# Sliding-window attention beside an MLP: fewer transfers for rows of maxima and outputs, and the last stage normalised a unit ahead

## The chip, the cores and the metric

The kernel runs on one core of a Trainium2 chip. Its metric is the device time of one execution in microseconds (us), the median of three runs. Five engines work side by side, each through its own queue in program order: PE (TensorE, matrix products; a matmul and the load of its weights are listed apart, as PE and PEld), DVE (VectorE), ACT (ScalarE), POOL (GpSimd) and SP (SyncE), which in this kernel only issues DMA transfers, all of them. An engine waits for another one by a semaphore; what stands behind a waiting instruction on the same engine waits with it.

## The reference

For x of shape [2048, 640], the layer norm `xn` of x goes two ways, and the result is `x + s * g`:

```python
qkv = (xn @ wqkv).reshape(B, S, 3, H, Dh)            # H = 32 heads of Dh = 20
scores = einsum("bhqd,bhkd->bhqk", q, k) * Dh ** -0.5
mask = (i - j >= 0) & (i - j < 256)                  # sliding window, causal
o = einsum("bhqk,bhkd->bhqd", softmax(where(mask, scores, -1e9)), v)
s = o.transpose(...).reshape(B, S, D) @ wo
h = relu(xn @ w1 + b1) ** 2                          # F = 1536
g = silu(h @ w2 + b2)
out = x + s * g
```

All inputs are float32. The kernel splits the operands of the large products into a rounded part (`fp32r`) and a remainder and sums three products of these, so that most products come in threes.

## The kernel before, in words

**Phase 1** normalises x in four blocks of 512 rows, transposes it, and makes v for all heads and q, k for the first head group. Results go to DRAM: q and k to `q_d`, `k_d`, v to `v_d`, the transposed x to `xs`.

**The attention** runs over 16 pairs of heads and, in each pair, 16 tiles of 128 query rows: 256 steps, and 11 more to drain. A step multiplies q with up to three tiles of keys (`sps`, L478), and DVE finds the maximum of each query (L486). Every fourth step (`max_rows`, L488) PE turns the maxima of four tiles into rows, ACT and POOL make a rounded row and a remainder of them (`mrow`, L500 and L501), and DMA writes these as two more rows under q for each head of the pair, in the tile `qs`. Nine steps later the scores are computed again with keys and queries exchanged (`stps`, L520); the two extra rows of q and rows of ones under k subtract the maximum in the product itself. ACT takes the exponential, POOL masks, and every fourth step `values` (L534) multiplies by v, with a column of ones that gives the sum of each softmax. For each of the two heads and for even and odd tiles the result `ot` lies in a group of 32 partitions, 21 of them used; ACT copies it to `osb`, and DMA takes it to `o_d`, one tensor for each block of 512 rows.

**The filler** puts everything else into the gaps of these steps: q and k of the other four head groups, then the MLP. The MLP has two halves of F and four blocks each; a block makes the hidden layer (`hps`) and then, for each of four tiles of rows and two halves of columns, a product `yps`, which DVE evicts with a sum (`ysb`, L953) to `y_d`. In the second half the first half's result comes back as `yin` (L877). A model clock orders the work: each product has a cost in `COST`, each group of value products `PV`, and `fill` issues filler products until the step's share of the model time is used up. The products are cut in two halves of 64 rows that run side by side on PE. A product needs one of three banks of PSUM, and the bank comes free by the eviction of the product that had it.

**The last stage** (`out_filler`, L1028) begins when the filler and all steps are through. It has eight units of 256 rows. `load` (L1000) brings a unit's attention output (`ob`), its softmax sums (`sums`, each row four times, since 128 partitions hold 32 heads four times over) and its MLP result (`yb`). `normalized` (L1034) takes the reciprocal, multiplies and splits in two pieces (DVE and ACT). Then for two tiles of 128 rows and two halves of columns 15 matmuls with `wo` fill a bank (`wops`, L602); DVE multiplies with the silu of `yb` (L1078), POOL adds x (L1079), and the row block goes out. `load` is called for units 0 and 1 in the last MLP block, after the second and the fourth of its tiles (L982). In the out stage, a unit is normalised ahead of the third of the four products of the unit before it; unit 0 is normalised at the start of the stage.

**Transfers on SP** stand in program order. `post` puts a transfer on a list and `post_all` (L567) issues the list: at the start of a step, after its filler work, and ahead of an eviction. Tiles have a fixed number of buffers; a transfer into one waits until its last reader is through.

## Time and profile before

| | |
|---|---|
| time, median of 3 runs | 927.04 us (922.24 to 929.7) |
| the profiled execution | 926.19 us, span 924.4 us |
| mean granted clock of PE | 0.983 |
| PE busy | 880.1 us (95%) |
| DVE, ACT, POOL busy | 498.9, 415.7, 327.1 us |
| moved by DMA | 165.76 MB, 179 GB/s over the span |
| transfers `qs<-mrow` | 256, 2 KB each |
| transfers `o<-osb` | 256, 21 KB each |
| transfers `sums<-o`, `ob<-o`, `yb<-y` | 32, 32 and 8 |

A row of the profile has the line, the engine, the operation, and the tiles as out<-in, with partitions x elements. The brackets at the end of a row in order of time give the idle time of the engine ahead of it and what ended it. A "granted clock" of 1.00 is the full clock of PE. Phase 1 takes about the first 115 us, the steps reach to about 800, and the last stage begins with the first `wops` at 831.9.

### The profile page before, as it was taken

How to read it: one execution, taken by the hardware profiler on the slowest of the kernel's cores; microseconds unless marked ns; L12 is line 12 of the kernel's file. 1: busy time of each engine (PE TensorE's matmuls, PEld its weight loads, DVE VectorE, ACT ScalarE, POOL GpSimd, SP SyncE). 2: the span in 40 equal slices, each digit the busy share in tenths (PEclk: the TensorE clock that was granted, in tenths of full speed). 3: DMA queues.
4: the chain of work that ended last, by engine and by line, in shares of the span. 5: the costliest groups of instructions: out<-in, count | busy, mean ns of one | idle time of the engine just before them, and what ended most of it. 6: DMA issues, size and time to landing. Idle time of an engine off the chain costs nothing. (4 is left out here: it accounts for less than half of the span.)

```text
span 924.4 us, 27328 instructions
## 1 busy us (share of the span) xinstructions
PE 880.1 (95%) x10640; PEld 815.5 (88%) x10640; DVE 498.9 (54%) x1446; ACT 415.7 (45%) x800; POOL 327.1 (35%) x702
## 2 busy tenths in 40 slices
PE   8999999999999999999999999999999999969887
PEld 8999999877878999989989899989899998958877
DVE  7652155655564655555555676745555653225664
ACT  4222125444454654644635656635635635502221
POOL 5010003232323543533534534534634534302223
PEclk9999999999998999999999999999999999988999
DMA  7996777677777453262365255465274532274984
GB/s 252 323 378 228 213 221 232 219 232 226 219 238 237 122 195 110 67 211 84 85 195 164 75 164 143 124 195 152 62 235 124 166 116 81 67 214 139 258 246 160
DMA packets 90825, 165.76 MB, mean 179 GB/s; under 512 B 11976, under 2 KB 46408, under 8 KB 88136
## 3 DMA queue, kind: packets, MB, share of 16 engines
q1 hardware_dynamic: 90696, 164.02, 57.2%
q8 instruction: 84, 1.38, 0.6%
q14 instruction: 45, 0.37, 0.1%
HBM read 94.71 MB, written 68.68 MB: 177 GB/s over the span
## 5 line engine op out<-in xcount | busy, mean ns | idle before, releaser
L486 DVE CUSTOM_DVE_ANT_0 junk<-sps,mask 128x384 bf16<-128x384 f32 (+2 forms) x512 | 271.8, 531 | 216.3 <-PE sps L478 82.9
L526 ACT ACTIVATE p<-stps 128x768 f32<-128x768 f32 (+2 forms) x256 | 197.1, 770 | 279.7 <-PE stps L520 234.3
L468 PE MATMUL yps<-w,hh 64*128 64x320 f32 x1536 | 231.4, 312 | 2.9 <-DVE sq L920 2.7
L527 POOL TENSOR_SCALAR_AFFINE_SELECT p<-p 128x256 f32<-128x256 f32 x256 | 104.6, 409 | 357.4 <-ACT p L526 354.2
L468 PE MATMUL hps<-xb,w 64*128 64x256 f32 x2520 | 220.7, 284 | 0.0
L468 PEld LDWEIGHTS hps<-xb,w 64*128 64x128 f32 x2520 | 207.9, 188 | 5.4 <-issue 5.1
L468 PEld LDWEIGHTS yps<-w,hh 64*128 64x128 f32 x1536 | 184.4, 186 | 8.2 <-DVE sq L920 4.6
L468 PE MATMUL yps<-w,hl 64*128 64x320 f32 x768 | 178.0, 311 | 0.0
L520 PE MATMUL stps<-qs,ks 62*128 62x384 f32 (+2 forms) x512 | 135.7, 339 | 15.5 <-DMA qs<-mrow 15.1
L478 PE MATMUL sps<-ks,qs 60*128 60x384 f32 (+2 forms) x512 | 139.1, 344 | 0.2
L468 PEld LDWEIGHTS yps<-w,hl 64*128 64x128 f32 x768 | 115.7, 186 | 2.5 <-issue 2.4
L520 PEld LDWEIGHTS stps<-qs,ks 62*128 62x128 f32 x512 | 86.6, 189 | 23.1 <-issue 16.1
L468 PE MATMUL qkps<-xT,wgkh 64*128 64x512 f32 x320 | 102.8, 406 | 0.0
L468 PE MATMUL qkps<-xT,wgqh 64*128 64x512 f32 x320 | 101.3, 398 | 0.0
L548 PE MATMUL ops<-p,vp 128*21 128x128 f32 (+1 forms) x2112 | 92.8, 313 | 0.0
L529 POOL TENSOR_SCALAR_AFFINE_SELECT p<-p 128x256 f32<-128x256 f32 x224 | 91.6, 409 | 0.0
L478 PEld LDWEIGHTS sps<-ks,qs 60*128 60x128 f32 x512 | 84.9, 187 | 2.9 <-DVE mt L486 1.7
L602 PE MATMUL wops<-wo,oT 128*128 128x320 f32 x384 | 69.4, 324 | 18.6 <-ACT oT L108 15.4
L548 PEld LDWEIGHTS ops<-p,vp 128*21 128x21 f32 x2112 | 65.2, 100 | 22.4 <-issue 9.5
L602 PEld LDWEIGHTS wops<-wo,oT 128*128 128x128 f32 x384 | 60.3, 196 | 23.9 <-ACT oT L108 17.9
L921 POOL TENSOR_TENSOR hl<-sq,hh 128x256 fp32r<-128x256 f32 x96 | 71.2, 744 | 23.1 <-DVE sq L920 20.5
L228 PE MATMUL vps<-wv,xT 128*128 128x320 f32 x480 | 71.5, 308 | 0.0
(99 smaller groups left out, 1221.1 us busy)
## 6 DMA issues: line engine op xcount, KB each, us to landing
ks<-k_d SPq DMA_DIRECT2D x64, 240.0 KB
qs<-q_d SPq DMA_DIRECT2D x64, 240.0 KB
xb<-xs SPq DMA_DIRECT2D x12, 1280.0 KB
xs<-xT SPq DMA_DIRECT2D x8, 1280.0 KB
y<-ysb SPq DMA_DIRECT2D x32, 320.0 KB
k_d<-shm SPq DMA_DIRECT2D x19, 512.0 KB
q_d<-shm SPq DMA_DIRECT2D x19, 512.0 KB
v_d<-vt SPq DMA_DIRECT2D x8, 672.0 KB
```

Source lines behind the costliest of these rows:

```text
L228: nc.tensor.matmul(ps, xT[xp][b][:, c * BT + t * P: c * BT + (t + 1) * P], wv[wp][:, c, nh * HALF:(nh + 1) * HALF], start=first and m == 0 ...
L468: return nc.tensor.matmul(out, a[r], b_[r], skip_group_check=True, **kw)
L478: nc.tensor.matmul(ss[hh][:, :nk], qs[i][o, q * P:(q + 1) * P], ks[i][o, k0 * P:k0 * P + nk], start=True, stop=True)
L486: nc.vector.tensor_tensor_reduce(out=junk[:, :nk], in0=ss[hh][:, :nk], in1=mask[:, 3 * P - nk:], scale=1.0, scalar=-3.0e38, op0=ALU.add, o ...
L520: nc.tensor.matmul(tps[:, hh, :n], ks[i][o, kb * P:(kb + 1) * P], qs[i][o, kb * P:kb * P + n], start=True, stop=True)
L526: nc.scalar.activation(p32[:, :, :n], tps[:, :, :n], AF.Exp, scale=SCALE)
L527: nc.gpsimd.affine_select(p32[:, :, 0:P], p32[:, :, 0:P], pattern=[[0, 2], [1, P]], compare_op=ALU.is_ge, fill=0.0, base=0, channel_multip ...
L529: nc.gpsimd.affine_select(p32[:, :, 2 * P:], p32[:, :, 2 * P:], pattern=[[0, 2], [-1, P]], compare_op=ALU.is_gt, fill=0.0, base=0, channel ...
L548: nc.tensor.matmul(ot[r0:r0 + VW, c0:c0 + len(part), :], vps[p][:, kb // 4, kb % 4, hh, :], pt[:, hh, :].rearrange("p (t n) -> p t n", n=P ...
L602: nc.tensor.matmul(ps, a, b_, start=j == 0, stop=j == n - 1)
L921: nc.gpsimd.tensor_sub(hh[1][:, sl], sq, f32(hh[0][:, sl]))
```

## The change

It has four parts.

1. The rows of maxima are written by two transfers for a group of four tiles, one for each of the two parts of `mrow`, each for both heads, and are issued at once instead of being posted.
2. The output of a block is written by one transfer of all 128 partitions, with the unused rows, into `o_d` of a new layout (row in the group, head, column). For that the groups of partitions in `ot` are exchanged: even and odd tiles of one head lie next to each other. So a unit is now two tiles of the same parity (`tile_of`), and its loads are three transfers instead of nine.
3. In the last MLP block `late` loads unit 0 at the start, and from the sixth of the eight products on issues the two pieces of unit 0's normalisation (`turn_out`) and the load of unit 1; it also takes up pieces of `wo`. In the last stage the two pieces of unit u+1 stand ahead of the first and the second product of unit u. The last tile's addition of x is on DVE.
4. `PV` is 1.57 instead of 1.65.

```diff
-PV = 1.65
+PV = 1.57
...
-    o_d = [dram.tile([H, VW, BT], F32, name=f"o_{g}") for g in range(NB)]
+    o_d = [dram.tile([2 * 32, H, MT], F32, name=f"o_{g}") for g in range(NB)]
...
-            for hh in range(2):
-                for a in range(2):
-                    o = hh * HP + KR + a
-                    post(f32(qs[i])[o:o + 1, g * 512:(g + 1) * 512].rearrange("r (q n) -> r q n", q=4), f32(mrow)[4 * hh:4 * hh + 4, a, :])
+            for a in range(2):
+                nc.sync.dma_start(f32(qs[i])[KR + a:KR + a + HP + 1:HP, g * BT:(g + 1) * BT].rearrange("h (q n) -> h q n", q=4), f32(mrow)[:, a, :])
...
-                    r0 = 32 * (hh + 2 * (t % 2))
+                    r0 = 32 * (2 * hh + t % 2)
...
-            for k in range(4):
-                post(o_d[g][2 * p + k % 2].rearrange("w (j e n) -> w j e n", j=2, e=2)[:, :, k // 2, :], osb[32 * k:32 * k + VW])
+            post(o_d[g][:, 2 * p:2 * p + 2, :].rearrange("r h n -> h r n"), osb.rearrange("p e n -> p (e n)"))
...
+        def late(j):
+            load(0)
+            if state[2] < 10 ** 6:
+                return
+            start_pieces()
+            for f in release(1, True):
+                f()
+                held[0] -= 1
+            if j >= 5:
+                turn_out(0, 0)
+            if j >= 6:
+                turn_out(0, 1)
+                load(1)
...
                 for nh in range(2):
                     yield from room()
+                    if n == last:
+                        late(2 * tt + nh)
                     job = start(nh)
...
-                if n == last and tt % 2:
-                    load(0)
-                    load(1)
...
+    def tile_of(u, t2):
+        return 4 * (u // 2) + u % 2 + 2 * t2
...
-        for k in range(4):
-            nc.sync.dma_start(sums[32 * k:32 * k + H], o_d[u // 2][:, DH, cols])
-            nc.sync.dma_start(ob[32 * k:32 * k + H], o_d[u // 2][:, k:DH:4, cols])
-        nc.sync.dma_start(yb, y_d[1][:, 2 * u:2 * u + 2, :])
+        rows = o_d[u // 2][32 * (u % 2):32 * (u % 2 + 1)]
+        nc.sync.dma_start(sums, rows[DH].unsqueeze(0).to_broadcast([4, H, MT]))
+        nc.sync.dma_start(ob, rows[:DH].rearrange("(c k) h n -> (k h) c n", k=4))
+        t = tile_of(u, 0)
+        nc.sync.dma_start(yb, y_d[1][:, t:t + 3:2, :])
...
+    def turn_out(u, part):
+        if (u, part) in turned_out or u not in ld:
+            return
+        turned_out.add((u, part))
+        ob, _, sums = ld[u]
+        if not part:
+            nc.vector.reciprocal(sums, sums)
+            big = bigp.tile([P, KC * BT], F32R, tag="big", name=f"oT_{u}")
+            oT[u] = big.rearrange("p (s c n) -> p s c n", s=2, c=KC)
+        cs = slice(2, KC) if part else slice(0, 2)
+        nc.vector.tensor_mul(ob[:, cs], ob[:, cs], sums.unsqueeze(1).to_broadcast([P, cs.stop - cs.start, MT]))
+        split(oT[u][:, 0, cs], oT[u][:, 1, cs], ob[:, cs])
...
-            if u not in oT:
-                flush()
-                normalized(u)
             flush()
+            turn_out(u, 0)
+            turn_out(u, 1)
...
-                    if t2 and not nh and u + 1 in ld:
+                    if not t2 and u + 1 in ld:
                         flush()
-                        normalized(u + 1)
+                        turn_out(u + 1, nh)
...
                         nc.vector.tensor_mul(res[:, sl], ps, yb[:, t2, sl])
+                        if t == NT - 1:
+                            nc.vector.tensor_add(res[:, sl], res[:, sl], xt[:, sl])
+                            post(out[t * P:(t + 1) * P, sl], res[:, sl])
+                            return
                         nc.gpsimd.tensor_add(res[:, sl], res[:, sl], xt[:, sl])
```

Three places show how it moves instructions. The first is the queue of SP in a block of four steps of the second phase, before (`raw` is a piece of MLP weights, `qs` and `ks` the tiles of q and k, `o_85` the output of the first block of rows):

```order
L756 DMA raw<-in_B_w_dram 128x640
L567 DMA o_85<-osb 42x1x128 x4
L567 DMA qs_1350<-mrow 1x4x128 x4
L567 DMA k_d<-shm 128x2x512
L567 DMA k_d<-slo 128x512
L684 DMA ks_1351<-k_d 60x1024
```

and the same block now:

```order
L753 DMA raw<-in_B_w_dram 128x640
L564 DMA o_85<-osb 2x64x256
L503 DMA qs_1350<-mrow 2x4x128 x2
L564 DMA k_d<-shm 128x2x512
L564 DMA k_d<-slo 128x512
L753 DMA raw<-in_B_w_dram 128x640
```

Three transfers stand where eight stood, in the same order. The second place is DVE at the end of the MLP, before (`wo_14774` and `wo4l` are remainders of `wo`, `ysb` the evictions of the last block's products):

```order
L777 TENSOR_TENSOR wo_14774<-raw,wo_14773 128x640
L953 TENSOR_TENSOR ysb<-yps,yin 128x320 x2
L777 TENSOR_TENSOR wo_14774<-raw,wo_14773 128x640
L953 TENSOR_TENSOR ysb<-yps,yin 128x320 x6
L777 TENSOR_TENSOR wo_14774<-raw,wo_14773 128x640
L777 TENSOR_TENSOR wo4l<-raw,wo4h 128x640
L1036 RECIPROCAL sums<-sums 128x256
L1041 TENSOR_TENSOR ob_14939<-ob_14939,sums 128x512
```

and now:

```order
L964 TENSOR_TENSOR ysb<-yps,yin 128x320 x2
L774 TENSOR_TENSOR wo_14461<-raw,wo_14460 128x640 x2
L774 TENSOR_TENSOR wo4l<-raw,wo4h 128x640
L1036 RECIPROCAL sums<-sums 128x256
L1040 TENSOR_TENSOR ob_14339<-ob_14339,sums 128x512
L109 TENSOR_TENSOR oT_14668<-ob_14339,oT_14668 128x512
L964 TENSOR_TENSOR ysb<-yps,yin 128x320
L1040 TENSOR_TENSOR ob_14339<-ob_14339,sums 128x768
L109 TENSOR_TENSOR oT_14668<-ob_14339,oT_14668 128x768
L964 TENSOR_TENSOR ysb<-yps,yin 128x320 x5
```

The first half of unit 0's normalisation and two remainders of `wo` stand ahead of the third eviction, the second half ahead of the fourth. The third place is DVE in the last stage, from one reciprocal on, before:

```order
L1036 RECIPROCAL sums<-sums 128x256
L1041 TENSOR_TENSOR ob_14939<-ob_14939,sums 128x512
L109 TENSOR_TENSOR oT_15217<-ob_14939,oT_15217 128x512
L1041 TENSOR_TENSOR ob_14939<-ob_14939,sums 128x768
L109 TENSOR_TENSOR oT_15217<-ob_14939,oT_15217 128x768
L1078 TENSOR_TENSOR res<-wops,yb_14940 128x320 x4
```

and now:

```order
L1036 RECIPROCAL sums<-sums 128x256
L1040 TENSOR_TENSOR ob_14339<-ob_14339,sums 128x512
L109 TENSOR_TENSOR oT_14833<-ob_14339,oT_14833 128x512
L1094 TENSOR_TENSOR res<-wops,yb_14340 128x320
L1040 TENSOR_TENSOR ob_14339<-ob_14339,sums 128x768
L109 TENSOR_TENSOR oT_14833<-ob_14339,oT_14833 128x768
L1094 TENSOR_TENSOR res<-wops,yb_14340 128x320 x3
```

An eviction (`res`) now stands between the two halves of a normalisation.

More of the change, by code (lines that the diff above doesn't have):

```diff
@@ L1007, in load @@
         sums = at2.tile([P, MT], F32, tag="sums", name="sums")
-        cols = slice(u % 2 * MT, (u % 2 + 1) * MT)
-        for k in range(4):
-            nc.sync.dma_start(sums[32 * k:32 * k + H], o_d[u // 2][:, DH, cols])
-            nc.sync.dma_start(ob[32 * k:32 * k + H], o_d[u // 2][:, k:DH:4, cols])
-        nc.sync.dma_start(yb, y_d[1][:, 2 * u:2 * u + 2, :])
-        ld[u] = (ob, yb, sums)
-    obs = {}
+        rows = o_d[u // 2][32 * (u % 2):32 * (u % 2 + 1)]
[3 more added lines that the diff above has]
+        nc.sync.dma_start(yb, y_d[1][:, t:t + 3:2, :])
+        ld[u] = (ob, yb, sums)
+    obs, oT, turned_out = {}, {}, set()
+    def turn_out(u, part):
[10 more added lines that the diff above has]
+        split(oT[u][:, 0, cs], oT[u][:, 1, cs], ob[:, cs])
     def queue_wo():
@@ L1028, in out_filler @@
     def out_filler(wo_part):
-        oT, xts = {}, {}
+        xts = {}
         def load_res(t):
@@ L1032, in load_res @@
             nc.sync.dma_start(xts[t], x[t * P:(t + 1) * P, :])
-        def normalized(u):
-            ob, _, sums = ld[u]
-            nc.vector.reciprocal(sums, sums)
-            big = bigp.tile([P, KC * BT], F32R, tag="big", name=f"oT_{u}")
-            oT[u] = big.rearrange("p (s c n) -> p s c n", s=2, c=KC)
-            for cs in (slice(0, 2), slice(2, KC)):
-                n = cs.stop - cs.start
-                nc.vector.tensor_mul(ob[:, cs], ob[:, cs], sums.unsqueeze(1).to_broadcast([P, n, MT]))
-                split(oT[u][:, 0, cs], oT[u][:, 1, cs], ob[:, cs])
         load_res(0)
@@ L1071, in out_filler @@
                     yield from mm_group(ps, mms, 0.133)
-                    if nh == 0 and t + 1 < NT:
-                        load_res(t + 1)
+                    if nh == 0 and t != NT - 1:
+                        load_res(tile_of(u, 1) if not t2 else tile_of(u + 1, 0))
                     load(u + 1)
@@ L1078, in evac @@
                         nc.vector.tensor_mul(res[:, sl], ps, yb[:, t2, sl])
+                        if t == NT - 1:
+                            nc.vector.tensor_add(res[:, sl], res[:, sl], xt[:, sl])
+                            post(out[t * P:(t + 1) * P, sl], res[:, sl])
+                            return
                         nc.gpsimd.tensor_add(res[:, sl], res[:, sl], xt[:, sl])
-                        if t == NT - 1:
-                            post(out[t * P:(t + 1) * P, sl], res[:, sl])
-                        elif nh:
+                        if nh:
                             post(out[t * P:(t + 1) * P, :], res)
```

2 lines of the change are left out of this document (1 added, 1 removed).

## The prediction

> **What bounds the kernel now.** I read the page's first two parts, then the groups of waits of the matrix engine, then the order of time at the places that these waits name, and last the stretches of 10 us with their clock.
>
> ```profile
> span 924.4 us, 27328 instructions
> PE 880.1 (95%) x10640; PEld 815.5 (88%) x10640; DVE 498.9 (54%) x1446; ACT 415.7 (45%) x800; POOL 327.1 (35%) x702
> ...
> PE wops L602 <- ACT oT L108: 15.4, 9, 9.0
> PE stps L520 <- DMA qs<-mrow: 15.1, 16, 2.2
> PE wops L602 <- DVE oT L109: 3.0, 7, 0.4
> ```
>
> PE (TensorE) is busy 95% of the span and every other engine about half of it, so time is won only where PE waits or runs below its clock. Only two kinds of wait are long (us in total, times, longest): the last stage waits for the normalised attention output, 15.4 + 3.0 us, and the transposed scores wait for the rows of maxima, 15.1 us in 16 waits of at most 2.2.
>
> Stage hand-over, in order of time (start, duration, what, and in brackets the idle time ahead):
>
> ```profile
> 809.80 0.44 SPq L1010 DMA_DIRECT2D sums<-o  x1
> ...
> 818.73 0.44 SPq L1012 DMA_DIRECT2D yb<-y  x1
> 820.13 0.34 SPq L877 DMA_DIRECT2D yin<-y  x1
> 826.26 0.89 DVE L953 TENSOR_TENSOR ysb<-yps,yin 128x320 f32<-128x320 f32 x2 [8.43 <-DMA y<-ysb]
> 828.71 1.75 DVE L1036 RECIPROCAL sums<-sums 128x256 f32<-128x256 f32 x1
> 831.90 2.16 PE L602 MATMUL wops<-wo,oT 128*128 128x320 f32 x6 [8.96 <-ACT oT L108]
> ```
>
> The 18 loads of units 0 and 1 hold the SP queue from 809.80 to 819.17. The `yin` of the last MLP tile comes behind them at 820.13, so DVE stands 8.43 us before the last two evictions, then starts the first normalisation, and PE has been idle for 8.96 us when its first product of the last stage starts.
>
> The same in a later unit, and the clock (columns: stretch, length, PE busy, granted clock, DMA share, GB/s):
>
> ```profile
> 841.43 1.74 DVE L1036 RECIPROCAL sums<-sums 128x256 f32<-128x256 f32 x1
> 905.68 1.74 DVE L1036 RECIPROCAL sums<-sums 128x256 f32<-128x256 f32 x1
> 849.26 1.92 PE L602 MATMUL wops<-wo,oT 128*128 128x320 f32 x12
> 851.46 0.75 PE L602 MATMUL wops<-wo,oT 128*128 128x320 f32 x4
> 50.00:60.00 10.00, 10.00 (x70) 1.00 1.07 384
> 240.00:250.00 10.00, 8.47 (x62) 0.83 0.61 203
> 270.00:280.00 10.00, 7.82 (x73) 0.85 0.63 199
> 290.00:300.00 10.00, 10.00 (x140) 0.83 0.77 252
> 600.00:610.00 10.00, 8.71 (x94) 0.83 0.97 301
> 770.00:780.00 10.00, 8.02 (x106) 0.83 0.09 22
> 830.00:840.00 10.00, 7.70 (x25) 0.50 0.41 126
> 860.00:870.00 10.00, 8.69 (x57) 1.00 0.90 242
> 890.00:900.00 10.00, 9.39 (x60) 1.00 0.83 260
> ```
>
> From the reciprocal of unit 1 to that of unit 7 are six units in 64.25 us, 10.71 each. A product is 15 matmuls, the 12 from 849.26 and three with `wo4` before the next product's at 851.46: 2.20 us, so the four of a unit take 8.80: PE stands 1.91 us in each unit. Clock losses lie in the five middle stretches at 0.83 to 0.85 and in 830 to 840 at 0.50.
>
> **The change part by part.** Hand-over. Of the 18 issues six remain, three for each unit, and unit 0's are placed at the start of the block instead of half-way; at 0.44 us each, unit 1's three hold SP 1.3 us instead of 4, and `yin` no longer comes late. Behind unit 0's three in the queue stand the last two `o` transfers and eight loads of `wo`, which may wait the 1.3 us, since `wo` is wanted only after the MLP. The loads themselves move the same rows: 128 of `sums`, now a row read four times by one transfer, 640 of `ob`, and `yb` in two pieces per partition. DVE's reciprocal, products and splits of unit 0 move between the evictions of the last block. There they are 1.75 + 0.69 + 0.69 + 0.95 + 0.96 = 5.0 us of DVE, from rows of the last stage:
>
> ```profile
> 862.78 1.74 DVE L1036 RECIPROCAL sums<-sums 128x256 f32<-128x256 f32 x1
> 864.55 0.69 DVE L1041 TENSOR_TENSOR ob<-ob,sums 128x512 f32<-128x512 f32 x1
> 865.99 0.69 DVE L109 TENSOR_TENSOR oT<-ob,oT 128x512 fp32r<-128x512 f32 x1 [0.75 <-ACT oT L108]
> 866.60 0.95 DVE L1041 TENSOR_TENSOR ob<-ob,sums 128x768 f32<-128x768 f32 x1
> 868.46 0.96 DVE L109 TENSOR_TENSOR oT<-ob,oT 128x768 fp32r<-128x768 f32 x1 [0.91 <-ACT oT L108]
> 811.33 0.49 DVE L953 TENSOR_TENSOR ysb<-yps,yin 128x320 f32<-128x320 f32 x1 [2.32 <-PE yps L468]
> 817.34 0.49 DVE L953 TENSOR_TENSOR ysb<-yps,yin 128x320 f32<-128x320 f32 x1 [2.87 <-PE yps L468]
> ```
>
> DVE stood idle for most of the time between these evictions, which follow their products (811.33 and 817.34 are two apart, so 3.0 us each), and that cover is used up. The third eviction now stands behind two weight remainders that came after all evictions (the 1.6 us between 827.15 and 828.71) and the first half of unit 0, 3.8 us from reciprocal to split: 5.4 us late at most, where the three banks let it be late by two products, 6.0. If that fails, PE stands a microsecond or two there. What is late next is the eviction of the last product, 0.5 us. So 8.96 becomes 0.5, bounds 0 and 3: **-8.4**.
>
> Clock behind the gap. PE runs at 0.50 from 831.90 to about 840.3; half of 8.1 us of work is lost. Without the gap it stays warm: **-4.0**, bounds 0 and -5.0, the loss of the whole stretch.
>
> The other seven units. The normalisation of unit u+1 now starts in front of unit u's first product instead of its third, its second half in front of the second. DVE's round is the 6.64 us from 862.78 to 869.42, with the ACT copies in it, and four evictions at 0.45: 8.4 against PE's 8.8. It fits with 0.4 to spare, so of 1.91 I leave 0.2: 7 x 1.7 = **-12**, bounds 0 and -13.4.
>
> Rows of maxima. The place in time:
>
> ```profile
> 267.42 0.45 POOL L501 TENSOR_TENSOR mrow<-row,mrow 8x128 fp32r<-8x128 f32 x1 [0.15 <-ACT mrow L500]
> ...
> 268.78 3.33 SPq L567 DMA_DIRECT2D o<-osb  x4
> 272.21 2.69 SPq L567 DMA_DIRECT2D qs<-mrow  x4
> ...
> 275.79 0.77 PE L520 MATMUL stps<-qs,ks 62*128 62x384 f32 x2 [2.18 <-DMA qs<-mrow]
> L567 SPq DMA_DIRECT2D qs<-mrow x256: 572/588/944, 128.7 to 782.9; - x128
> L567 SPq DMA_DIRECT2D o<-osb x256: 738/768/1395, 157.2 to 809.0; - x128
> ```
>
> The rows were ready at 267.87; PE had them at 275.79. In between SP issued eight small transfers, 6.0 us, and 0.9 us after the last issue the data was there. After the change it is one `o` and two `mrow`: 0.77 + 2 x 0.59 + 0.9 = 2.8 us instead of 7.0, if a transfer of the new shape costs what one of the old does. That isn't shown: the new `o` transfer is 64 rows of 1 KB for each of two heads, 131 KB, where the four had 86. Bounds for it: 0.77, and 1.4, the slowest of 256. Also the first `mrow` now waits in the queue itself and not in the list of posts; behind it stand the `k_d`, `q_d` stores and later loads, which nothing on PE waits for. A gain of 4 us exceeds the longest wait, 2.2; I leave 2 us for those in which a bulk load lies ahead: **-13**, bounds 0 and -15.1.
>
> The clock in the middle: 10 x (0.17 + 0.15 + 0.17 + 0.17 + 0.17) = 8.3 us. All five stretches hold or follow waits for `mrow`; one I leave: **-6.6**, bounds 0 and -8.3. [...]
>
> End: the last addition goes from POOL to DVE, with these rows
>
> ```profile
> 920.31 0.49 DVE L1078 TENSOR_TENSOR res<-wops,yb 128x320 f32<-128x320 f32 x1 [1.65 <-PE wops L602]
> 920.88 0.85 POOL L1079 TENSOR_TENSOR res<-res,xres 128x320 f32<-128x320 f32 x1 [1.26 <-DVE res L1078]
> ```
>
> 0.85 becomes 0.49: **-0.4**. The lower PV shifts few products across the value products (193 instead of 189 halves are left behind the last of them, some 0.3 us) and is set at nothing.
>
> Sum: -8.4 - 4.0 - 12 - 13 - 6.6 - 0.4 = -44.4. The profiled execution took 926.19 (span 924.4 and 1.8 around it), which gives 881.8; the median of the three runs, 927.04, is 0.85 above it. I say **882**.
>
> **Rivals.** First, the large `o` transfer stands in the way of the rows behind it. At 50 to 60 the 16 DMA engines moved 384 GB/s, 24 each. Should the transfer lie on two of them, because its outer extent is two heads, 131 KB take 2.7 us, and `mrow` behind it on the same engines lands after 5.5 us, not 2.8. That is still below 7.0. If small rows go at half that rate, 5.5 us, the landing is at 8.3, the waits stay and both middle terms vanish: 882 + 19.6 = 902. [...] No view here shows the spread.
>
> Second, the other side, the same place taken further. In the stretch 200 to 300
>
> ```profile
> 200.00:300.00 100.00, 93.15 (x1003) 81.85 (x1003) 56.52 (x170) 49.93 (x91) 28.89 (x75) 0.95 0.74 233
> ```
>
> the DMA share is 0.74. The rows of maxima come 64 times between 128.7 and 782.9, every 10.4 us, so each engine has 2.7 us free in a block, just what two engines at 24 GB/s need. At 12 they need 5.5 and run over by 2.8 us in each of the 16 blocks up to 300, in which the stores and loads of q and k are spread over all engines and wait for the slowest: +45, and with the lost middle terms 947. It ends above 926 from 1.5 us over per block, 16 GB/s per engine.
>
> Third, the last stage meets another bound. Each unit moves 640 + 128 + 640 KB in and 640 KB each of x and output, 2.75 MB; in 8.8 us that is 313 GB/s. The stage showed 242 to 260 at a share of 0.83 to 0.90. If 260 is its ceiling, a unit takes 10.6, the 12 us are lost, 894. Against it stands the 384 of the first phase, though with larger rows; DVE's round of 8.4 would give the same if evictions waited for `res` buffers.
>
> Fourth, the head start does not work: DVE's work beside the MLP holds up the evictions, PE stands there instead of later, and the 12.4 us of gap and clock stay: 894. Last, the five slow stretches have another cause than the waits and stay: 889.
>
> **How the numbers follow.** The forecast gets 0.54, with its own range 870 to 893: all waits gone and the clock warm give 876, less if SP's relief ends small waits elsewhere; half of a large term lost gives the upper end. The first rival 0.11, the third 0.11, the fourth 0.06, the clock's own cause 0.07; slower 0.07, and 0.04 that these waits only move and nothing changes. The range 868 to 906 takes in all but the last two. Within 1% (917.8 to 936.3) is about what a measurement of this kernel can't tell from no change; chances 0.89 faster, 0.04 same, 0.07 slower.
>
> **What would show it.** Right: no wait of PE for `oT` above 1 us and none ahead of the first `wops`; that product at clock 1.00; reciprocals 8.8 to 9.2 apart; PE's waits for `mrow` below 3 us in total; no middle stretch at 0.83. Wrong: waits for `mrow` of 2 us and more with SP idle (first rival), DMA share above 1 and waits for `k_d` or `xb` (second), DVE `res` waiting for `out` in each unit (third), `yps` products waiting for a bank (fourth).

## The result, and the profile after

The changed kernel takes **883.78 us** (median, 882.05 to 884.48), 0.954 of the time before, with an interval of 0.950 to 0.958. The forecast was 882. The profiled execution has a span of 880.3 us, 882.1 with what lies around it, 44.1 below that of before; the sum was -44.4. By the medians of the same runs the difference is 42.4 (926.2 before), since the profiled execution is the fastest of the four. The sum came out, but not each of its terms: two errors of 3.6 and 3.9 us cancel, which is luck, and two terms of the last stage were right for reasons that the prediction gave only in part.

The busy times of the changed kernel, and two of PE's waits (total us, times, longest):

```profile
PE 860.6 (98%) x10640; PEld 802.6 (91%) x10640; DVE 498.7 (57%) x1448; ACT 414.8 (47%) x800; POOL 329.9 (37%) x700
...
PE stps L518 <- DMA qs<-mrow: 5.7, 8, 1.7
PE yps L468 <- DVE ysb L964: 0.9, 2, 0.7
```

PE is busy 98% of the span instead of 95%. The 18.4 us of waits for `oT` are gone. Of the 15.1 us for the rows of maxima, 5.7 are left, in 8 waits instead of 16.

The hand-over to the last stage, in order of time:

```profile
785.26 0.57 SPq L1022 DMA_DIRECT2D sums<-o  x1
...
786.94 0.67 SPq L1025 DMA_DIRECT2D yb<-y  x1
794.44 0.33 SPq L874 DMA_DIRECT2D yin<-y  x1
787.01 1.75 DVE L1036 RECIPROCAL sums<-sums 128x256 f32<-128x256 f32 x1
...
803.45 1.74 DVE L1036 RECIPROCAL sums<-sums 128x256 f32<-128x256 f32 x1
...
858.08 1.74 DVE L1036 RECIPROCAL sums<-sums 128x256 f32<-128x256 f32 x1
791.33 0.56 PE L468 MATMUL yps<-w,hh 64*128 64x320 f32 x4 [0.71 <-DVE ysb L964]
794.47 0.56 PE L468 MATMUL yps<-w,hh 64*128 64x320 f32 x4 [0.23 <-DVE ysb L964]
803.68 1.99 PE L599 MATMUL wops<-wo,oT 128*128 128x320 f32 x12 [0.68 <-DVE ysb L964]
```

Unit 1's three loads hold SP from 785.26 to 787.61, and DVE normalises unit 0 from 787.01, sixteen microseconds ahead of the stage. PE pays 0.71 + 0.23 us for a bank, and has a gap of 0.68 instead of 8.96. From the reciprocal of unit 1 to that of unit 7 are six units in 54.63 us, 9.1 each instead of 10.71.

The same stretches of 10 us as before (length, PE, PEld, DVE, ACT and POOL busy, granted clock, DMA share, GB/s):

```profile
240.00:250.00 10.00, 10.00 (x122) 8.46 (x120) 6.65 (x20) 5.70 (x11) 3.48 (x9) 1.00 1.00 287
270.00:280.00 10.00, 10.00 (x150) 9.29 (x150) 7.22 (x22) 6.29 (x11) 3.48 (x9) 1.00 0.84 297
290.00:300.00 10.00, 9.81 (x162) 9.03 (x160) 8.18 (x22) 7.57 (x17) 5.54 (x11) 1.00 0.19 60
600.00:610.00 10.00, 10.00 (x160) 9.50 (x157) 5.20 (x19) 3.98 (x7) 3.63 (x10) 1.00 0.63 174
770.00:780.00 10.00, 9.68 (x128) 8.87 (x126) 2.67 (x5) 6.83 (x15) 4.89 (x11) 1.00 0.51 164
830.00:840.00 10.00, 9.98 (x69) 9.75 (x68) 7.73 (x13) 2.64 (x3) 5.02 (x6) 1.00 0.94 287
870.00:880.00 10.00, 6.03 (x40) 5.50 (x38) 3.40 (x6) 0.00 (x0) 1.72 (x2) 0.93 0.47 167
```

No stretch but the last is below 1.00. The first `wops` comes at 803.68 instead of 831.90: of these 28.2 us the gap gave 8.3 and the part ahead of it (called the middle below) 19.9. From there to the end it takes 76.6 us instead of 92.5.

### The profile page after: what moved, and what is told of

It is laid out like the page before. It is cut to its first block, busy times and chain, and to the rows that moved or that the text cites. A ratio compares the mean times of both kernels' runs of the same rounds, so it can differ in the third digit from the quotient of the medians.

```text
span 880.3 us, 26692 instructions
## 1 busy us (share of the span) xinstructions
PE 860.6 (98%) x10640; PEld 802.6 (91%) x10640; DVE 498.7 (57%) x1448; ACT 414.8 (47%) x800; POOL 329.9 (37%) x700
## 4 chain that ended last, share of the span: by engine, by line
PE 76%; DMA 11%; ACT 4%; DVE 4%; issue 3%; POOL 2%; SPq 0%; DVEq 0%; POOLq 0%; ACTq 0%
PE yps L468 16%; PE hps L468 16%; PE qkps L468 13%; PE ops L546 8%; PE vps L228 8%; DMA qs<-mrow 5%; PE stps L518 4%; PE sps L478 4%; PE qkps L205 3%; DMA out_dram<-res 3%; POOL res L1099 2%; PE wops L599 1%; DMA ks<-k_d 1%; ACT p L524 1%; ACT relu L926 1%
## 5 line engine op out<-in xcount | busy, mean ns | idle before, releaser
L468 PE MATMUL hps<-xb,w 64*128 64x256 f32 x2520 | 218.2, 283 | 0.0
L468 PEld LDWEIGHTS yps<-w,hh 64*128 64x128 f32 x1536 | 188.8, 185 | 9.7 <-DVE sq L931 4.8
L468 PE MATMUL yps<-w,hl 64*128 64x320 f32 x768 | 182.8, 309 | 0.0
L518 PE MATMUL stps<-qs,ks 62*128 62x384 f32 (+2 forms) x512 | 130.1, 335 | 5.8 <-DMA qs<-mrow 5.7
L468 PEld LDWEIGHTS yps<-w,hl 64*128 64x128 f32 x768 | 121.6, 185 | 2.1 <-issue 2.1
L468 PE MATMUL qkps<-xT,wgkh 64*128 64x512 f32 x320 | 100.9, 395 | 0.0
L468 PE MATMUL qkps<-xT,wgqh 64*128 64x512 f32 x320 | 99.4, 393 | 0.0
L518 PEld LDWEIGHTS stps<-qs,ks 62*128 62x128 f32 x512 | 83.4, 187 | 8.7 <-issue 7.7
L228 PEld LDWEIGHTS vps<-wv,xT 128*128 128x128 f32 x480 | 70.5, 188 | 0.1
L931 DVE SCALAR_TENSOR_TENSOR sq<-hps,b1t,relu 128x256 f32<-128x256 f32 x96 | 46.2, 482 | 39.2 <-ACT relu L926 39.1
```

Source lines behind the costliest of these rows:

```text
L228: nc.tensor.matmul(ps, xT[xp][b][:, c * BT + t * P: c * BT + (t + 1) * P], wv[wp][:, c, nh * HALF:(nh + 1) * HALF], start=first and m == 0 ...
L468: return nc.tensor.matmul(out, a[r], b_[r], skip_group_check=True, **kw)
L518: nc.tensor.matmul(tps[:, hh, :n], ks[i][o, kb * P:(kb + 1) * P], qs[i][o, kb * P:kb * P + n], start=True, stop=True)
L931: nc.vector.scalar_tensor_tensor(sq, ps.tile[:, sl], b1t[:, fi + i:fi + i + 1], r, ALU.add, ALU.mult)
```

## The experiments

In the table, "middle ends" is the start of the first `wops` less the idle time ahead of it, from each kernel's own profile; "waits" is PE's total for `qs<-mrow`. The ratio is to executions of the kernel before in the same series as each kernel's (their medians lie between 925.88 and 931.03), with its interval. A profile is of one execution: that of the change is its fastest, that of the kernel with one transfer a head its slowest (877.06).

| kernel | time, us | ratio | middle ends | waits, us |
|---|---|---|---|---|
| before | 927.04 | 1 | 822.9 | 15.1 |
| the change | 883.78 | 0.954 (0.950 to 0.958) | 803.0 | 5.7 |
| rows alone | 903.27 | 0.974 (0.969 to 0.979) | 799.1 | 6.3 |
| output transfers alone | 917.50 | 0.989 (0.984 to 0.995) | 814.8 | 11.8 |
| a unit ahead alone | 908.84 | 0.981 (0.975 to 0.987) | 826.9 | 14.6 |
| no head start | 889.35 | 0.960 (0.954 to 0.966) | 802.2 | 6.2 |
| one transfer a head | 874.04 | 0.944 (0.942 to 0.946) | 798.0 | 0.3 |
| heads outside | 884.21 | 0.955 (0.953 to 0.957) | 793.4 | none |
| rows posted | 885.43 | 0.957 (0.954 to 0.960) | 803.4 | 5.9 |
| PV 1.65 | 884.89 | 0.954 (0.951 to 0.957) | 804.6 | 5.4 |
| halves of the columns | 893.13 | 0.966 (0.963 to 0.969) | 814.0 | 12.7 |
| a head, output first | 873.07 | 0.943 (0.940 to 0.946) | 796.6 | 0.6 |
| a head, first in the last unit | 872.95 | 0.944 (0.941 to 0.947) | 794.4 | 0.3 |
| the same, four loads | 883.59 | 0.952 (0.947 to 0.956) | 794.1 | none |

### One part at a time

**Rows of maxima alone.** The kernel before with

```diff
-            for hh in range(2):
-                for a in range(2):
-                    o = hh * HP + KR + a
-                    post(f32(qs[i])[o:o + 1, g * 512:(g + 1) * 512].rearrange("r (q n) -> r q n", q=4), f32(mrow)[4 * hh:4 * hh + 4, a, :])
+            for a in range(2):
+                nc.sync.dma_start(f32(qs[i])[KR + a:KR + a + HP + 1:HP, g * BT:(g + 1) * BT].rearrange("h (q n) -> h q n", q=4), f32(mrow)[:, a, :])
```

> The kernel before with part 1 of the change alone: two transfers for the rows of maxima, issued at once; four posted output transfers as before. Theory A (the SP queue made the rows late, and the output transfer on two engines is what keeps the 5.7 us of waits in the changed kernel): the rows go out ahead of the four small output transfers and nothing large lies before them, so PE's waits for mrow fall from 15.1 to 3 us or less, the stretches at 0.83 go, and the time is 15 to 20 us below before, 907 to 911. Theory B (the remaining 5.7 us come from bulk loads and stores ahead of the rows, not from the output transfer): waits of 5 to 7 us as in the changed kernel, time 910 to 913. Rival C (the slow stretches have another cause than the waits): the waits fall, the clock stays at 0.83 to 0.85 in five stretches, 915 to 919.

903.27 us, 24.3 below before and below the ranges of all three theories; the middle alone ends 23.8 us earlier. But 6.3 us of waits stay, where theory A said 3 or less. One of the places, in order of time:

```profile
267.74 0.45 POOL L501 TENSOR_TENSOR mrow<-row,mrow 8x128 fp32r<-8x128 f32 x1
268.07 3.33 SPq L565 DMA_DIRECT2D o<-osb  x4
271.44 0.47 SPq L682 DMA_DIRECT2D qs<-q_d  x1
272.02 1.27 SPq L503 DMA_DIRECT2D qs<-mrow  x2
274.96 0.45 PE L518 MATMUL stps<-qs,ks 62*128 62x384 f32 x2 [1.48 <-DMA qs<-mrow]
```

The rows are ready at 268.19 and go out at 272.02, behind the four output transfers that SP is still issuing; 1.7 us after their last issue PE has them. So what is left at this place is SP's queue, and neither bulk transfers (theory B) nor the large output transfer, which this kernel does not have. Of the 23.8 us, 8.8 are waits and 8.3 the clock of the slow stretches; the other 6.7 have no row of their own and stay open.

**Output transfers alone**: the second part of the change without the others.

> The kernel before with part 2 alone: one output transfer per block, the new layout of o_d, three loads per unit, units of tiles of one parity; rows of maxima in four posted transfers, normalisation as before. Theory A: SP is relieved of three issues per block (2.2 us) but the rows stand behind a transfer on two engines that takes 5.4 us to land; the two about cancel and the waits for mrow stay at 10 to 18 us; the hand-over gap falls by the 12 issues saved there from 8.96 to 4 or 5 us, with part of the half clock: 915 to 922. Theory B (the output transfer does not matter for the rows): waits for mrow fall to 9 or less and the slow stretches shrink, 905 to 912.

917.50 us, as theory A had it, with waits of 11.8 us and a middle shorter by 8.1. The gap ahead of the stage did not fall to 4 or 5; its row:

```profile
806.65 1.25 SPq L876 DMA_DIRECT2D yin<-y  x1
817.73 0.89 DVE L952 TENSOR_TENSOR ysb<-yps,yin 128x320 f32<-128x320 f32 x2 [8.02 <-DMA y<-ysb]
823.37 2.16 PE L601 MATMUL wops<-wo,oT 128*128 128x320 f32 x6 [8.55 <-ACT oT L108]
```

SP issues `yin` here 8.2 us ahead of the gap (which begins at 814.82) and not 2.8, yet DVE stands 8.02 us ahead of the last two evictions, much as before. By the completion events of the trace (a transfer has several; the last is taken as its landing) `yin` lands at 816.79 and the store `y<-ysb` behind it at 817.61: ahead of them the DMA engines work through the loads of both units, issued one behind the other, at a share of 1.03 from 808 to 814; the last of these lands at 815.99. Twelve fewer issues gain nothing at this place; what holds `yin` back is the bytes ahead of it.

**A unit ahead alone**: the third part, with the old transfers and nine loads for a unit.

> The kernel before with part 3 alone: unit 0 loaded at the start of the last MLP block and normalised beside it, every later unit a unit ahead, last addition on DVE; transfers, layout and PV as before (nine loads per unit). The forecast's sum for this part: gap -8.4, half clock behind it -4.0, seven pauses -12, end -0.4, in all -24.8: 901 to 904. If the nine loads per unit still hold the SP queue when yin is wanted, the gap stays at 4 us or more and the time is 906 to 910. The waits for mrow stay at 15 us and the slow middle stretches stay at 0.83.

908.84 us, 18.7 below the kernel before of the same runs (927.53) instead of 24.8. Three rows of the hand-over and one of the units (60 us in one stretch):

```profile
810.84 0.48 DVE L967 TENSOR_TENSOR ysb<-yps,yin 128x320 f32<-128x320 f32 x1
814.49 0.34 SPq L877 DMA_DIRECT2D yin<-y  x1
811.38 0.90 PE L468 MATMUL yps<-w,hh 64*128 64x320 f32 x4 [2.57 <-DVE ysb L967]
830.00:890.00 60.00, 56.44 (x377) 54.98 (x376) 39.80 (x54) 16.06 (x19) 24.50 (x24) 1.00 0.96 267
```

The gap ahead of the first `wops` is 0.7 us, so the nine loads do not bring it back: `yin`, at 814.49, comes early enough. PE stands 2.57 us for a bank instead: the third eviction, at 810.84, is on DVE behind the last remainder of `wo` and the first half of unit 0's normalisation. The clock is at half for the 10.2 us from 810.2 to 820.4. The units follow each other every 9.96 us (reciprocals at 827.31 and 887.08), with the DMA engines 0.96 busy at 267 GB/s: nearly a full load, for 6% fewer bytes a second than the 285 GB/s of the change (its row stands further below). That looks like the third rival of the forecast, a ceiling near 260; in this kernel it is read from the share, not tested.

**Without the head start.** The changed kernel, unit 0 normalised at the start of the stage:

```diff
-            if j >= 5:
-                turn_out(0, 0)
             if j >= 6:
-                turn_out(0, 1)
                 load(1)
```

> The changed kernel without the head start beside the MLP: unit 0 is loaded at the start of the last block as in the change, but its reciprocal, products and splits come at the start of the last stage; later units a unit ahead as in the change. Forecast's theory: PE stands for what DVE and ACT need from the last eviction to the first half of unit 0, about 1.75 + 0.69 + 0.75 + 0.69, some 4 us, and the clock falls behind it as it did before: +4 to +9 over the changed kernel, 888 to 893. If a gap of 4 us costs no clock: 887 to 888. If the early yin alone were what closed the gap: 884 to 885.

889.35 us, 5.6 above the change and as the forecast's theory had it. Its gap and the two stretches behind it:

```profile
805.78 2.16 PE L599 MATMUL wops<-wo,oT 128*128 128x320 f32 x6 [3.63 <-ACT oT L108]
800.00:810.00 10.00, 5.96 (x26) 4.68 (x25) 6.21 (x8) 3.25 (x4) 0.00 (x0) 0.72 0.27 73
810.00:820.00 10.00, 10.00 (x56) 10.00 (x56) 5.77 (x10) 3.41 (x4) 3.28 (x3) 0.77 0.60 176
```

With unit 0's loads at the start of the block, far ahead of unit 1's, the gap falls from 8.96 to 3.63 with no help from the head start; the head start is worth the rest of the gap and half clock behind it.

### What is left of the waits

**One transfer for each head.** In the changed kernel,

```diff
-            post(o_d[g][:, 2 * p:2 * p + 2, :].rearrange("r h n -> h r n"), osb.rearrange("p e n -> p (e n)"))
+            for hh in range(2):
+                post(o_d[g][:, 2 * p + hh, :], osb[HP * hh:HP * (hh + 1)].rearrange("p e n -> p (e n)"))
```

> The changed kernel, with the output of a block written by two transfers, one for each head (64 partitions to 64 rows), instead of one whose outermost extent is two; loads and layout as in the change. Theory A (the output transfer lies on two DMA engines and the rows of maxima stand behind it there): with 64 as outermost extent it is spread, the rows land in about 2.4 us instead of 3 to 6, PE's waits for mrow fall from 5.7 to about 3, the last product of the MLP ends 3 to 4 us earlier (799 instead of 803), time 879 to 881. Theory B (the remaining waits come from bulk loads, the transfer costs nothing): waits stay at 5 to 6.5, time 883 to 885, or up to 1 us more for the second issue.

874.04 us, 9.7 below the change. The waits are theory A's, and the time is below its range of 879 to 881:

```profile
PE stps L518 <- DMA qs<-mrow: 0.3, 1, 0.3
```

The same group of rows in the changed kernel (first four lines) and here (the last two):

```profile
657.02 0.52 SPq L564 DMA_DIRECT2D o<-osb  x1
659.38 1.12 SPq L503 DMA_DIRECT2D qs<-mrow  x2
659.49 0.45 POOL L501 TENSOR_TENSOR mrow<-row,mrow 8x128 fp32r<-8x128 f32 x1 [0.15 <-ACT mrow L500]
666.60 0.44 PE L518 MATMUL stps<-qs,ks 62*128 62x384 f32 x2 [0.97 <-DMA qs<-mrow]
```

```profile
654.09 1.16 SPq L565 DMA_DIRECT2D o<-osb  x2
656.45 1.24 SPq L503 DMA_DIRECT2D qs<-mrow  x2
```

In the change SP issues the rows by 660.50, and PE gets them at 666.60, six microseconds later; by the completion events the output transfer ahead of them lands at 665.95 and the rows at 666.47. Here the rows had landed at 658.97, 1.3 us after their issue, and PE does not wait at all. Over all 64 groups those events give a median of 3.8 us from issue to landing for a row transfer of the change and 1.7 here; for the output transfer 5.4 and 2.7. In the two profiles the waits differ by 5.4 us and the end of the middle by 5.0. The medians lie 9.7 apart; what makes the rest, besides the choice of the executions, is open.

**Halves of the columns**: also two transfers, each still with two heads as its outermost extent.

```diff
-            post(o_d[g][:, 2 * p:2 * p + 2, :].rearrange("r h n -> h r n"), osb.rearrange("p e n -> p (e n)"))
+            for e in range(2):
+                post(o_d[g][:, 2 * p:2 * p + 2, e * P:(e + 1) * P].rearrange("r h n -> h r n"), osb[:, e, :])
```

> The changed kernel with the output of a block in two transfers by halves of the columns; each still has two heads as its outermost extent, 64 rows of 512 bytes each. It has the two issues of the version with one transfer for each head, and not its outer extent. Theory A (the outermost extent of two puts the transfer on two DMA engines, and that is the price): waits for mrow stay at 5 to 7 us, time 883 to 886, 9 to 12 above the version for each head. Theory B (two smaller transfers let the rows pass between them, whatever engines they are on): waits of 2 us or less, 874 to 879.

893.13 us, on theory A's side and beyond its numbers:

```profile
PE stps L518 <- DMA qs<-mrow: 12.7, 11, 2.2
```

Issues and bytes are those of the version for each head, and the difference is 19 us. So the outermost extent decides, and not the number of transfers: rows of 1 KB with an extent of two are slow in the change as well. To cut the transfer without changing the extent is worse than to leave it whole. Why is not shown: now 256 rows of 512 bytes go where 128 of 1 KB went, but from the first issue to the last landing the pair takes 5.5 us (median) where the whole transfer takes 5.4.

**Heads outside.** One transfer of 128 rows into one piece of DRAM, and `ob` loaded by four transfers:

```diff
-    o_d = [dram.tile([2 * 32, H, MT], F32, name=f"o_{g}") for g in range(NB)]
+    o_d = [dram.tile([H, 2 * 32, MT], F32, name=f"o_{g}") for g in range(NB)]
...
-            post(o_d[g][:, 2 * p:2 * p + 2, :].rearrange("r h n -> h r n"), osb.rearrange("p e n -> p (e n)"))
+            post(o_d[g][2 * p:2 * p + 2].rearrange("h r n -> (h r) n"), osb.rearrange("p e n -> p (e n)"))
...
-        nc.sync.dma_start(ob, rows[:DH].rearrange("(c k) h n -> (k h) c n", k=4))
+        for k in range(4):
+            nc.sync.dma_start(ob[32 * k:32 * k + H], rows[:, k:DH:4])
```

> The changed kernel with the outputs stored head by head (head outside the row in the group): the output of a block is one transfer of 128 rows of 1 KB into one piece of DRAM, and a unit's attention output is loaded by four transfers instead of one (six for a unit instead of three). Theory A: as with one transfer for each head, waits for mrow about 3, and one issue less: 878 to 881. Theory B: 883 to 885. If the six loads of a unit hold the SP queue in the last stage: gap or pauses there, 884 to 888.

884.21 us: no wait for the rows is left, the middle ends at 793.4, and the last stage gives all of it back. Its units take 11.25 us (reciprocals from 793.80 to 861.30); a stretch of it, and the like of the change:

```profile
800.00:860.00 60.00, 51.41 (x330) 49.66 (x329) 35.01 (x48) 14.64 (x17) 20.94 (x22) 0.97 1.02 240
```

```profile
805.00:860.00 55.00, 54.59 (x370) 53.99 (x369) 39.76 (x56) 15.85 (x18) 24.49 (x24) 1.00 0.91 285
```

The DMA engines are full (share 1.02) at 240 GB/s, where the change moves 285 at 0.91. Two things differ, the four loads and the place of the rows in DRAM. To tell them apart, the version for each head (with the output first in the last unit) got the four loads and kept its layout:

```diff
-        nc.sync.dma_start(ob, rows[:DH].rearrange("(c k) h n -> (k h) c n", k=4))
+        for k in range(4):
+            nc.sync.dma_start(ob[32 * k:32 * k + H], rows[k:DH:4].rearrange("c h n -> h c n"))
```

> The version with one output transfer for each head and the output sent first in the last unit (872.95), with a unit's attention output loaded by four transfers of 32 partitions instead of one of 128; layout in DRAM as in the change. The version with the heads outside had these four loads and another layout, and its units took 11 us. If the four loads are the cause (their shape or the issues): units of 10 to 11.5 us, share of the DMA engines above 1 at 230 to 260 GB/s, 880 to 890. If the layout is the cause (where the rows lie in DRAM): units of 8.8 to 9.3, 873 to 876.

883.59 us, 10.6 above the same kernel with one load:

```profile
PE wops L600 <- DVE res L1099: 8.8, 8, 2.6
800.00:860.00 60.00, 52.69 (x341) 51.11 (x340) 36.48 (x50) 14.98 (x17) 22.93 (x24) 0.97 1.01 245
```

It is the four loads: units of 10.7 us (794.55 to 858.97). They move the same 640 rows of 1 KB. The issues alone do not explain it, since the pieces themselves take longer: in the trace's list of DMA packets those of 1 KB take 85 ns in the units here (median), and 46 in the same kernel with one load. What about 32 partitions in place of 128 takes the engines longer is open.

**Rows posted** (`post` in place of `nc.sync.dma_start`) and **PV 1.65**, both in the changed kernel:

> The changed kernel with the two transfers of the rows of maxima put on the list again instead of being issued at once. If the gain in the middle comes from having fewer issues, waits for mrow stay at 5 to 7 and the time is 883 to 886. If it comes from issuing at once, the rows go out up to a step's filler work later (about 2 us) and behind the output transfer: waits 9 to 13 us, some stretches at 0.83 again, 888 to 895.

> The changed kernel with PV at 1.65 as before. The forecast set this part at nothing: 883 to 885, same waits. If the lower PV itself shifts work so that the middle loses or gains: more than 1 us of difference, with the waits for mrow changed by as much.

885.43 and 884.89 us, with waits of 5.9 and 5.4: neither can be told from the change. Once there are few issues on SP in this kernel, it matters little whether the rows are issued at once; the 888 to 895 expected for that case did not come. But the profile of PV at 1.65 shows a pause of PE at the hand-over that the change does not have:

```profile
PE yps L468 <- DVE ysb L964: 2.3, 1, 2.3
790.00:800.00 10.00, 9.91 (x82) 9.72 (x84) 3.15 (x6) 3.40 (x3) 0.00 (x0) 0.66 0.36 107
```

It is the pause of the kernel with a unit ahead alone, 2.57 us and half clock, here with three loads for a unit. These two kernels have the head start and PV at 1.65; in all others with the head start PV is 1.57, and PE's waits for such a bank come to 0.9 to 1.1 us. So the pause goes with PV and not with the nine loads. The median does not show it: either other executions do without it (the fastest, 878.74 us, had a mean clock of 1.00), or PV at 1.65 gains as much elsewhere. Which of the two is open.

**The end of the last stage.** In the changed kernel DVE waits near the end:

```profile
860.45 7.45 SPq L1059 DMA_DIRECT2D xres<-in_A_x_dram  x2
867.95 1.63 SPq L564 DMA_DIRECT2D out_dram<-res  x2
873.56 1.28 DVE L1094 TENSOR_TENSOR res<-wops,yb 128x320 f32<-128x320 f32 x3 [6.18 <-DMA out_dram<-res]
```

SP stands with two loads of x that wait for POOL, the output behind them comes late, and DVE has no buffer for `res`. In the version for each head, the finished tile is evicted and sent ahead of that load:

```diff
-                    if not t2 and u + 1 in ld:
+                    if t2 or u == 2 * NB - 1:
+                        flush()
+                        post_all()
+                    elif u + 1 in ld:
                         flush()
                         turn_out(u + 1, nh)
```

and in a second kernel the same in the last unit alone.

> One output transfer for each head, and in the last stage the rows of a finished tile are evicted and sent ahead of the next load of x for every second tile of a unit and throughout the last unit. In the changed kernel DVE waits 6.18 us near the end for a transfer of output that stands on SP behind two loads of x. Theory: PE loses some 2 us of the last unit to that; without it 872 (1 to 2 us below the version for each head). If the earlier wait of SP for POOL holds up the loads of the unit after next instead: pauses in the units, 875 to 880.

> One output transfer for each head, and the output sent ahead of the next load of x in the last unit alone. The order of transfers on SP stays the same up to there, so that nothing else can be held up: 872 to 873 if the wait near the end costs PE 1 to 2 us, 874 if it costs nothing or if the transfer that DVE waits for was put on the list before this place.

873.07 and 872.95 us, 1.0 and 1.1 below the version for each head and inside its interval. In the profile of the first, PE does not stand at all through the units:

```profile
800.00:855.00 55.00, 55.00 (x377) 55.00 (x376) 40.14 (x55) 16.12 (x19) 24.28 (x24) 1.00 0.93 296
```

Both are 11 us faster than the change, with intervals that do not meet its own; nearly all of that is the output transfer.

## Why the prediction was right, by its steps

| term | forecast | measured |
|---|---|---|
| gap at the hand-over | -8.4 | -8.3 |
| clock behind it, units, end | -16.4 | -15.9 |
| waits for the rows | -13 | -9.4 |
| slow stretches of the middle | -6.6 | -8.3, and 2.2 more |
| sum | -44.4 | -44.1 |

**Hand-over and clock behind it: right in size, the cause half right.** The third eviction of the last block was to be late by little; PE paid 0.94 us in two waits for a bank. Without the head start the change loses 5.6 us. But the forecast put the late `yin` down to the 18 issues on SP. With six issues at the old place `yin` goes out 8.2 us ahead of the gap instead of 2.8, and the gap is still 8.55, since the loads of both units are ahead of it on the DMA engines; with unit 0's loads moved to the start of the block it is 3.63, with the head start too 0.68, and with both and all 18 issues (a unit ahead alone) 0.7. So their place counted, which the forecast also named, and not their number.

**The seven units: the number right, the step incomplete.** 9.1 us lie in the range of 8.8 to 9.2. But the forecast said of the new loads that they "move the same rows", and gave them no term. With loads of the old kind the units take 9.96 (a unit ahead alone) and, in four transfers, 10.7 (last row of the table), with the DMA engines at a share of 0.96 and 1.01 and at 267 and 245 GB/s. Without the one load of 128 partitions the third rival, which gave 10.6 us for a unit, would have come true, at 10 us of cost. What the prediction held against that rival, the 384 GB/s of the first phase, did not decide it; the one load in place of four did.

**Rows of maxima: the term mis-sized.** The step that failed is "a gain of 4 us exceeds the longest wait, 2.2; I leave 2 us". SP's relief was as forecast: at the place shown, the first of the two transfers is issued at 659.38, before POOL has begun the second part of the rows. What it left out of the sum, the first rival named: the output transfer with an outermost extent of two holds back the rows behind it. Of its 5.7 us of waits, 0.3 stay when each head has its own transfer, and 12.7 stand when the two transfers keep the extent of two. That rival's mechanism is real: the output transfer lands 5.4 us after its issue (median), and 5.5 us for it was the case in which the rival had both terms of the middle vanish, 902. What it had wrong is that then all the waits stay: PE waits 8 times in the 64 groups, and 16 times before. Its price is 9.7 us by the medians, half of the 19.6 that it was given. The trace shows how little of such a transfer is on the way at once. In its list of DMA packets 61 of the 64 can be told from other transfers: 128 packets of 1 KB each, 46 ns a packet (median), at most four at once, 3.4 us from the first to the last (median; 2.7 to 4.7). The shortest takes what the rival reckoned for two engines, 2.7. The first load of `ob` in the change has 640 packets of that size, and up to 21 at once. A transfer's completion comes in several events in the traces: 16 for the output of one head, 3 for that of the change and for the halves of the columns, 8 for one of the four small transfers before, 5 and 3 for a row transfer before and after. The change's own load of `sums`, with an outermost extent of four, has 5 such events; what that costs the last stage was not tried.

**The slow stretches: right, and a little larger than forecast.** All five are at 1.00 after the change. In the kernel with the rows alone no stretch of 10 us between 110 and 800 is below it either, and with a unit ahead alone, where the waits stay, all five are at 0.83 to 0.93. With the output transfers alone (waits of 11.8 us) two places are at half clock, with the halves of the columns (12.7) two. So they come with the waits, against the last rival, though not with each wait. The 2.2 us beside them in the table have no row of their own. Waits of 2.2 us at most were enough for the five of the kernel before, and the last section shows a case with less.

**The slower side did not come**: the DMA share stays at or below 1.00 in the stretches above, and no product waits for stores or loads of q and k. **PV at nothing** fits the medians, but in the profiles the lower PV saves 1.4 us of waits for a bank at the hand-over and the half clock around them; whether it costs as much elsewhere is open. **The end**: DVE's wait of 6.18 us for a buffer was not foreseen; to send the output first gave about 1 us less, which can't be told from nothing.

One more point: the parts do not add up. Alone they give 24.3, 10.0 and 18.7 us against the kernel before of the same runs, 53 together; the change has 43. Rows and output transfers both shorten SP's queue, and with both the output transfer becomes what the rows wait for: from the moment the rows are made, their last issue is over after 3.7 us before (median), 2.3 and 1.9 with one of the two parts, 0.5 with both, but they have landed after 4.8, 3.6, 3.7 and again 3.7.

## What to carry to other kernels

When small transfers on the path are late, look at two places: how long they stand in the issuing queue (behind 6.0 us of issues at the place that the prediction shows), and what large transfer lies ahead of them on the DMA engines (5.7 us of waits behind one transfer for two heads, 0.3 behind one for each head); merging transfers mends the first and can make the second. Keep the outermost extent of a merged transfer large, on both sides: here an extent of two in DRAM cost 9.7 us, with 128 partitions on the other side. Load all 128 partitions in one transfer where the stage is near the DMA engines' limit: four loads instead cost 10.6 us, at a share of 1.01. Ahead of a transfer that is wanted soon, count the bytes that the DMA engines still have to move and not only the issues: twelve issues fewer left a wait of 8.02 us where there had been 8.43. Judge a merged transfer by the wait of the one behind it, not by its own landing: the halves of the columns land after 5.5 us where the whole lands after 5.4, and PE waits 12.7 us instead of 5.7.

## What the runs showed of the hardware

In these traces the clock falls at another time than the wait, and after less than a long one. The kernel before, in stretches of 1 us around its wait of 2.18 us that ends at 275.79:

```profile
274.00:275.00 1.00, 0.00 (x0) 0.00 (x0) 0.86 (x3) 0.00 (x0) 0.00 (x0) 1.00 0.04 12
275.00:276.00 1.00, 0.21 (x1) 0.18 (x1) 0.14 (x2) 0.00 (x0) 0.00 (x0) 1.00 0.07 25
276.00:277.00 1.00, 1.00 (x9) 0.88 (x10) 0.00 (x0) 0.40 (x1) 0.00 (x0) 0.96 1.03 385
277.00:278.00 1.00, 1.00 (x8) 1.00 (x6) 0.00 (x0) 0.68 (x2) 0.52 (x2) 0.50 1.03 330
...
280.00:281.00 1.00, 1.00 (x11) 1.00 (x10) 0.78 (x4) 0.64 (x1) 0.00 (x0) 0.83 0.83 218
```

During the wait the clock is 1.00; it falls at 276.9, when PE works again, and is back at about 280.3, some 3.4 us later: 1.7 us lost, nearly as much as the wait (around the 2.57 us of the kernel with a unit ahead alone it is 10.2 us at half). The length of a wait does not tell whether this happens: the 1.74 us that the change waits up to 595.69 cost no clock, while in the version for each head two stretches with 1.06 us of idle time in all did:

```profile
510.00:511.00 1.00, 0.30 (x2) 0.04 (x1) 1.00 (x4) 0.61 (x1) 0.29 (x1) 1.00 0.00 0
511.00:512.00 1.00, 0.64 (x3) 0.38 (x5) 0.86 (x5) 0.00 (x0) 1.00 (x3) 1.00 0.74 120
514.00:515.00 1.00, 1.00 (x11) 1.00 (x10) 0.48 (x3) 0.00 (x0) 0.10 (x1) 0.50 0.75 178
```

The records of the granted clock tell more. From 100 us on, the stretches at half clock of a profile begin whole multiples of 3.413 us apart (in the kernel before at 242.79, 276.93, 290.58, 604.61, 775.27 and 826.47, which are 10, 14, 106, 156 and 171 of them behind the first), and up to the last instructions they last 3.41 us or two to four times that. Cut along this grid from 120 us on, the fourteen profiles have 3089 windows of 3.413 us at full clock with a whole one behind them. The 16 in which PE is busy for 1.9 us or less are all followed by half clock; of the other 3073 only 9 are, and why these are stays open. The wait of 1.74 us lies across the edge of two windows, at 595.26, and leaves PE busy for 2.10 us of the first. So in these profiles half clock mostly goes with much idle time in one window, and not with a long wait.
